# Sixteen weight slots moved to sixteen different offsets modulo 512 bytes in a fused attention and MoE kernel

## The chip, the cores and the metric

The kernel runs on one core of one Trainium2 chip. The metric is the device time of one execution in microseconds (us). Before the change it is 1794.76 us, the median of two runs (1793.05 and 1796.48).

## The reference

Three layers follow each other. First, attention over pooled keys and values, for 8 batches of 8 heads, 576 positions and 64 channels. Its result, as 4608 tokens of 512 channels, goes through two feed-forward layers.

```python
k_p = k.reshape(B, H, Sp, pool, D).mean(axis=3); v_p = v.reshape(B, H, Sp, pool, D).mean(axis=3)
scores = scale * np.matmul(q, k_p.transpose(0, 1, 3, 2))
attn = np.exp(scores - max); attn = attn / (sum + 1e-09)
x = np.matmul(attn, v_p)            # 4608 x 512, float32
h = x @ w_in                        # 512 x 2048 (float64 weights)
x = (h * np.cos(h)) @ w_out         # 2048 x 512
g = x @ w_gate; val = x @ w_val     # 512 x 1536 each
out = ((g * sigmoid(g)) * val) @ w_out2   # 1536 x 512, float32
```

## The kernel before

The program has two stages on one core. Nearly all matmuls have float32r operands. A number is split into a high part, the cast to float32r, and a low part, the rest. A product of two split numbers takes three matmuls: high times high, high times low, low times high.

Stage 1 (lines 1140 to 1234) runs over 9 blocks of 512 tokens and, within a block, over 16 slices of 128 hidden channels. `pe_h` (lines 545 to 554) computes a slice's hidden values: for each of 4 chunks of input channels three matmuls (lines 551, 552, 553), whose weights lie in the tile `wa[j, c]` and whose moving operand is the split input `xhl`. `pe_y` (lines 605 to 622) adds the slice's part of the output; its weights are in `wo` or `wo_ring`, its moving operands are the tiles `gh` and `gl`. In block 0 it uses plain float32 operands (line 613), and each of these matmuls shows in the trace as two instructions. The attention of the following batches is spread over the slots (`run_slot`), with its own small matmuls on lines 310, 363, 373 and 395.

Stage 2 (`fpair`, line 813, and `out_phase`, line 898) computes the second feed-forward layer by a scheme of seven products in place of eight, over five pairs of token halves: three with halves of 512 tokens, two with 384. Its weights are pieces of 128 x 1024 float32 (512 KB). Each of the 84 pieces of a pass is used in 12 matmuls (line 805, or line 935 for the last product), whose moving operand is one of the tiles `t_P`, `xhl` or `op`. The pieces are made once, in the first pass, stored to DRAM (`piece_store`, line 706) and loaded again for each later use (`piece_load`, line 700).

The weights of line 551 to 553 and the pieces of stage 2 live in the same sixteen buffers, called slots here: the pool `wts` with the sixteen tags `wa00` to `wa33`. A slot is 128 partitions by 4096 bytes. The tags are laid out in the order in which the program first asks for them: wa00 to wa03, wa10 to wa12, wa30 to wa32, wa20 to wa22, wa13, wa23, wa33. Before they are weights, slots also take raw `w_in` chunks (`cv_load`, line 469) and the raw keys and values of batch 1 (`load_kv1`, line 191). In stage 2 piece number r takes slot r modulo 16 (line 697), and SyncE's queue issues the load of piece r + 16 when piece r has been used (line 868).

Where things lie: every tile that lies between `xhl`, `gh`, `gl` and the slots is a whole multiple of 512 bytes in size, and so is a slot. All sixteen slots, `xhl`, `gh`, `gl`, the tiles `t_P` and `op`, and (with an unused tile of 224 bytes, `pad_1`) `wo_ring` therefore begin at the same offset modulo 512 bytes, 256. A block of weights for one matmul is 128 columns of 4 bytes, 512 bytes of a partition; it begins at a multiple of 512 bytes from its slot's start. So does each chunk of a moving tile. One kind of float32r matmul is laid out otherwise: on line 395 the weights of head pair p are 512 bytes after those of pair p - 1, but its moving operand `pth` is 1280 bytes after, so that the distance between the two, modulo 512, is 0 for an even pair and 256 for an odd one.

Of the kernel before, what the change touches and what calls it, by code (L numbers as in the profile page):

```python
# [8 lines left out]
F32 = mybir.dt.float32  # L9
F32R = mybir.dt.float32r  # L10
# [15 lines left out]
def fused_kernel(  # L26
# [23 lines left out]
    P = 128  # L50
# [5 lines left out]
    TB = 512  # L56
# [15 lines left out]
    dram = ctx.enter_context(tc.tile_pool(name="dram", bufs=1, space=bass.MemoryType.DRAM))  # L72
    psum = ctx.enter_context(tc.tile_pool(name="psum", bufs=1, space=bass.MemoryType.PSUM))
    wts = ctx.enter_context(tc.tile_pool(name="wts", bufs=1, reuse_waits="tile"))
    p1w = tc.alloc_tile_pool(name="p1w", bufs=2, side="right", reuse_waits="tile")
    p1a = tc.alloc_tile_pool(name="p1a", bufs=1, reuse_waits="tile")

# [46 lines left out]
    def raw_tile(nm):  # L124
        return chain.tile([P, 2, TB], F32, name=nm, tag="raw", bufs=2)
# [65 lines left out]
    def load_kv1():  # L191

        for g in range(3):
            t = wts.tile([P, 2, TB], F32, name=f"k1_{g}", tag=f"wa3{g}")
            kraw1.append(t if g < 2 else t[: SL * NP])
            if g < 2:
                for x in range(2):
                    nc.sync.dma_start(t[x * SM : (x + 1) * SM], kview[1][g, x])
            else:
                for r in range(2):  # L200
                    nc.sync.dma_start(t[: SL * NP, r], kleft[1][r])
        for j in range(0, NP + 1, 2):
            t = wts.tile([P, 2, TB], F32, name=f"v1_{j}", tag=f"wa2{j // 2}")
            for r in range(2):
                rows = t[r * SM : (r + 1) * SM]
                if j < NP:
                    nc.sync.dma_start(rows, vview[1][r, :, j : j + 2])
                else:
                    nc.sync.dma_start(rows[:, 0], vleft[1])
            vraw1.append((j, t[:, : min(2, NP + 1 - j)]))  # L210
# [256 lines left out]
    cv = {}  # L467

    def cv_load(key, src, home=None):
        st = raw_tile(f"st_{key}") if home is None else wts.tile([P, 2, TB], F32, name=f"st_{key}", tag=home)  # L470
        st = st.rearrange("p a t -> p (a t)")
        nc.sync.dma_start(st.bitcast(U64), src)
        cv[key] = st.rearrange("p (t two) -> p t two", two=2)

# [12 lines left out]
    def cv_sign(key):  # L487
        st, ce = cv[key]
        cu = ce.bitcast(U32)
        nc.vector.scalar_tensor_tensor(  # L490
            out=cu, in0=st.bitcast(U32)[:, :, 1], scalar=0x80000000, in1=cu, op0=ALU.bitwise_and, op1=ALU.bitwise_or
        )

    def cv_high(key):
        hi = cv[key][0].bitcast(U32)[:, :, 1]
        nc.vector.tensor_scalar(hi, hi, 0xFFFFF, 0x100000, op0=ALU.bitwise_and, op1=ALU.bitwise_or)

    def cv_low(key):
        st = cv[key][0]
        bits = st.bitcast(U32)  # L500
        nc.vector.scalar_tensor_tensor(
            out=st[:, :, 1], in0=bits[:, :, 0], scalar=2.0**-32, in1=bits[:, :, 1], op0=ALU.mult, op1=ALU.add
        )

    def cv_mul(key):

        st, ce = cv.pop(key)
        scale = 2.0**-20 * (INV_2PI if key[0] == "i" else 1.0)
        nc.vector.scalar_tensor_tensor(out=ce, in0=st[:, :, 1], scalar=scale, in1=ce, op0=ALU.mult, op1=ALU.mult)
        return ce  # L510
# [24 lines left out]
    wa = {}  # L535
# [128 lines left out]
    SLOTS = [f"wa{j}{c}" for j in range(NG1) for c in range(KC)]  # L664
    NS = len(SLOTS)
    wc_dram = dram.tile([PIECES, P, 2 * TB], F32, name="wc_dram")
    pieces = {}
# [26 lines left out]

    def piece_tile(r):

        pieces[r] = wts.tile([P, 2, 2, 2, P], F32R, name=f"wc_{r}", tag=SLOTS[r % NS])
        return pieces[r]

    def piece_load(r):  # L700
        if r >= PIECES * len(PAIRS) or r < NI * NQ:
            return
        t = piece_tile(r)
        nc.sync.dma_start(t.rearrange("p a b c d -> p (a b c d)").bitcast(F32), wc_dram[r % PIECES])
# [13 lines left out]
    def gen_steps(i):  # L718

        ts = {prod: piece_tile(i * NQ + n) for n, prod in enumerate(PRODUCTS)}  # L720
        for kind in range(2):
            t = w2raw.pop((i, kind))
# [241 lines left out]
    def load_i(m):  # L964
        for _ in range(m):
            u = next(to_load_i, None)
            if u is not None:
                _, j, c = order[u]
                cv_load(keys[u], w_in[c * P : (c + 1) * P, j * TB : (j + 1) * TB], f"wa{j}{c}")

    def load_o(m):
        for _ in range(m):
            u = next(to_load_o, None)
            if u is not None:
                f = order[u][2]
                cv_load(keys[u], w_out[f * P : (f + 1) * P, :])
# [4 lines left out]
    def first(u):  # L981
        kind, j, c = order[u]
        while keys[u] not in cv:
            (load_o if kind == "o" else load_i)(1)
        if kind == "o":
            ce = wo_raw[c // 8][:, c % 8]
        elif u < KC + LEAD:
            ce = None
        else:
            ce = wo_raw[1][:, 4 + (u if u < KC + LEAD else u // 2) % 4]  # L990
        cv_exp(keys[u], ce)
        cv_bias(keys[u])

    def conv():

        n = len(order)
        begun = 0
        x = None
        done = -1
        for u in range(n + 1):  # L1000
            if u < n:
                while begun <= u:
                    first(begun)
                    begun += 1
                    yield done
                cv_sign(keys[u])
                yield done
            if u > 0:
                x = cv_mul(keys[u - 1])
                if order[u - 1][0] == "o":  # L1010
                    load_o(1)
                    done = u - 1
                else:
                    _, j, c = order[u - 1]
                    home = wa[j, c] = wts.tile([P, 2, TB], F32R, name=f"wa_{j}_{c}", tag=f"wa{j}{c}")
                    nc.scalar.copy(home[:, 0], x)
                yield done
            if u < n:
                cv_high(keys[u])
                yield done  # L1020
            while begun < min(u + 3, n, ahead[0]) and not (order[begun][0] == order[begun - 1][0] == "o"):
                first(begun)
                begun += 1
                yield done
            if u < n:
                cv_low(keys[u])
                yield done
            if u > 0 and order[u - 1][0] == "i":
                nc.vector.tensor_sub(home[:, 1], x, home[:, 0])
                done = u - 1  # L1030
                yield done

    wo_raw = []
    conv_ops = conv()
    conv_done = [-1]
    ahead = [2 * KC]
# [32 lines left out]
    prep_k(0)  # L1069
    load_i(3)  # L1070
    load_kv1()
    fill(8)
    do_qt(0, 0)
# [61 lines left out]
    def w2_get():  # L1135
        cv_load(f"w2_{w2g[0]}", w2_src(w2g[0]))
        w2g[0] += 1
# [7 lines left out]
    for i, s in enumerate(slots):  # L1145
        n, f = s
# [159 lines left out]
```

## Time and profile before

| | |
|---|---|
| runs shown | 1793.05 and 1796.48 us, median 1794.76 us |
| profiled execution: span from first to last instruction | 1797.6 us (its own time is not listed apart) |
| matmul instructions | 8076, busy 1745.5 us, 97% of the span |
| weight loads | 8076, busy 1449.9 us, 81% |
| VectorE, ScalarE, GpSimd | 68%, 56%, 8% |
| DMA | 357.00 MB, mean 199 GB/s |

PE is TensorE's matmul side and PEld its weight loads, which overlap the matmuls. A matmul's duration in the trace includes the time from its first column to its last result, so matmuls that follow each other overlap; what one costs is read from the distance between starts. In the view of the chain, each entry runs until the next begins, so an entry of 24 matmuls gives 24 such distances.

### The profile page before, as it was taken

Reading aid. Unit: us, or ns where it says so; the run is one execution under the profiler, and the core shown is the slowest. Engines: PE = TensorE matmul, PEld = TensorE weight load, DVE = VectorE, ACT = ScalarE, POOL = GpSimd, SP = SyncE. Lnnn points to the kernel's source line nnn. Section 1 sums busy time; section 2 is a strip of 40 time slices with the busy share of each in tenths; the row PEclk is TensorE's granted clock in tenths of the full one; section 3 lists DMA queues with packets and bytes.
Section 4 is the critical chain, followed back from the end, with each engine's and each line's share of the span. In section 5 each row is a group of like instructions: output and inputs, shape, how many; then the busy total and the mean of one; then the engine's idle time right before and its main releaser. Section 6 shows DMA issues by size and latency. Waiting matters only on the chain.

```text
span 1797.6 us, 23341 instructions
## 1 busy us (share of the span) xinstructions
PE 1745.5 (97%) x8076; PEld 1449.9 (81%) x8076; DVE 1230.6 (68%) x2142; ACT 1002.4 (56%) x1815; POOL 134.8 (8%) x218
## 2 busy tenths in 40 slices
PE   4889999999999999999999999999999999999998
PEld 3556587888888878788888888888888888999998
DVE  6697687867777677687776586863684367458447
ACT  5577477766766767677565564533443344344333
POOL 0140500403103021000000000000000000000000
PEclk9899999999999999999999999999999999999999
DMA  9534244646566464574885488576667556787783
GB/s 235 159 115 111 85 161 142 203 130 203 143 210 220 109 208 126 158 244 137 235 278 183 169 310 290 192 260 218 192 201 265 197 190 221 298 254 249 291 255 92
DMA packets 240244, 357.00 MB, mean 199 GB/s; under 512 B 141696, under 2 KB 147840, under 8 KB 240128
## 3 DMA queue, kind: packets, MB, share of 16 engines
q1 hardware_dynamic: 235440, 354.35, 61.8%
q10 hardware_dynamic: 4688, 1.18, 0.3%
q8 instruction: 64, 1.05, 0.2%
q14 instruction: 52, 0.43, 0.1%
HBM read 285.74 MB, written 69.73 MB: 198 GB/s over the span
## 4 chain that ended last, share of the span: by engine, by line
PE 85%; DMA 6%; DVE 5%; issue 2%; ACT 1%; SPq 0%; ACTq 0%; POOL 0%; DVEq 0%; POOLq 0%
PE X L805 15%; PE oX L935 8%; PE Y L805 7%; PE h L551 7%; PE h L552 6%; PE h L553 6%; PE acc L620 6%; PE acc L621 6%; PE acc L622 6%; PE oY L935 4%; PE Z L805 4%; PE av L395 3%; PE acc L613 2%; PE oZ L935 2%; PE s L310 2%
## 5 line engine op out<-in xcount | busy, mean ns | idle before, releaser
L551 PE MATMUL h<-xhl,wa 128*128 128x512 f32 x576 | 233.7, 406 | 5.7 <-DVE w L587 5.7
L805 PE MATMUL X<-t_P,wc 128*128 128x512 f32 (+1 forms) x1080 | 233.0, 368 | 1.6 <-ACT u L854 1.6
L552 PE MATMUL h<-xhl,wa 128*128 128x512 f32 x576 | 228.0, 396 | 0.0
L553 PE MATMUL h<-xhl,wa 128*128 128x512 f32 x576 | 226.6, 393 | 0.0
L805 PEld LDWEIGHTS X<-t_P,wc 128*128 128x128 f32 x1080 | 196.5, 188 | 28.5 <-ACT u L854 3.3
L620 PE MATMUL acc<-gh,wo_ring 128*128 128x512 f32 x448 | 178.9, 399 | 0.0
L621 PE MATMUL acc<-gl,wo_ring 128*128 128x512 f32 x448 | 174.9, 390 | 0.1
L622 PE MATMUL acc<-gh,wo_ring 128*128 128x512 f32 x448 | 174.7, 390 | 0.0
L561 ACT ACTIVATE w<-h,few 128x512 f32<-128x512 f32 x144 | 98.7, 686 | 102.5 <-PE h L553 94.2
L551 PEld LDWEIGHTS h<-xhl,wa 128*128 128x128 f32 x576 | 109.6, 190 | 33.3 <-DVE w L587 7.5
L587 DVE SCALAR_TENSOR_TENSOR w<-w,h 128x512 f32<-128x512 f32 x144 | 98.1, 682 | 48.9 <-ACT w L584 47.2
L552 PEld LDWEIGHTS h<-xhl,wa 128*128 128x128 f32 x576 | 109.6, 190 | 24.0 <-issue 2.6
L553 PEld LDWEIGHTS h<-xhl,wa 128*128 128x128 f32 x576 | 109.4, 190 | 23.8 <-issue 0.5
L562 DVE SCALAR_TENSOR_TENSOR w<-w,h 128x512 f32<-128x512 f32 x144 | 98.0, 680 | 33.9 <-ACT w L561 33.3
L598 ACT CAST gh<-w 128x512 fp32r<-128x512 f32 x128 | 79.0, 617 | 72.2 <-DVE w L587 63.8
L857 DVE TENSOR_TENSOR p<-p,X 128x512 f32<-128x512 f32 (+1 forms) x60 | 37.8, 632 | 116.9 <-PE X L805 107.9
L583 ACT ACTIVATE w<-w 128x512 f32<-128x512 f32 x144 | 90.8, 632 | 47.5 <-DVE w L562 45.8
L601 DVE TENSOR_TENSOR gl<-w,gh 128x512 fp32r<-128x512 f32 x128 | 90.2, 704 | 30.0 <-ACT gh L598 28.1
L128 ACT CAST xhl<-pst 128x1024 fp32r<-128x1024 f32 (+1 forms) x70 | 67.7, 967 | 71.4 <-PE oX L935 26.1
L935 PE MATMUL oX<-xhl,wc 128*128 128x512 f32 (+1 forms) x480 | 102.8, 368 | 0.0
L622 PEld LDWEIGHTS acc<-gh,wo_ring 128*128 128x128 f32 x448 | 84.1, 188 | 18.5
L620 PEld LDWEIGHTS acc<-gh,wo_ring 128*128 128x128 f32 x448 | 84.1, 188 | 17.2 <-issue 0.8
(203 smaller groups left out, 3476.9 us busy)
## 6 DMA issues: line engine op xcount, KB each, us to landing
wc<-wc_dram SPq DMA_DIRECT2D x273, 512.0 KB
wo_ring<-wo_dram SPq DMA_DIRECT2D x112, 512.0 KB
wc_dram<-wc SPq DMA_DIRECT2D x42, 512.0 KB
wc_dram<-ow SPq DMA_DIRECT2D x42, 256.0 KB
y_dram<-yo SPq DMA_DIRECT2D x18, 512.0 KB
w_dram<-ce_w SPq DMA_DIRECT2D x36, 256.0 KB
st_i<-in_moe_w_in_dram SPq DMA_DIRECT2D x16, 512.0 KB
st_o<-in_moe_w_out_dram SPq DMA_DIRECT2D x16, 512.0 KB
```

The costliest lines, as they stand in the source:

```text
L551: nc.tensor.matmul(ps, whi, xhl[0][:, 0, c], start=c == 0, stop=False)
L552: nc.tensor.matmul(ps, whi, xhl[0][:, 1, c], start=False, stop=False)
L553: nc.tensor.matmul(ps, wlo, xhl[0][:, 0, c], start=False, stop=c == KC - 1)
L561: nc.scalar.activation(w, h, AF.Identity, bias=magic)
L562: nc.vector.scalar_tensor_tensor(out=w, in0=w, scalar=MAGIC, in1=h, op0=ALU.subtract, op1=ALU.subtract)
L583: nc.scalar.activation(w, w, AF.Sin, scale=PI)
L587: nc.vector.scalar_tensor_tensor(out=w, in0=w, scalar=1.0, in1=h, op0=ALU.subtract, op1=ALU.mult, reverse0=True)
L620: nc.tensor.matmul(acc[n][i], a[:, cols], xh, start=f == 0, stop=False)
L621: nc.tensor.matmul(acc[n][i], a[:, cols], xl, start=False, stop=False)
L622: nc.tensor.matmul(acc[n][i], b[:, cols], xh, start=False, stop=f == NF1 - 1)
L805: nc.tensor.matmul(ps[:, :hb], w, t[:, x, c, :hb], start=first and c == 0 and n == 0, stop=c == 1 and n == 2, skip_group_check=not first,)
L935: nc.tensor.matmul(banks[key][m][:, :hb], u, x[:, b, i, :hb], start=first_ and j == i == k == 0, stop=j == NJ - 1 and i == 1 and k == 2, s ...
```

## The change

The sixteen slots get 32 more bytes each (1032 columns of 4 bytes in place of 1024). A slot's contents begin at its start, except for the slots wa01, wa11, wa21 and wa31, where they begin 16 bytes later. Relative to before, and modulo 512, the slots then begin at: wa00 0, wa01 48, wa02 64, wa03 96, wa10 128, wa11 176, wa12 192, wa30 224, wa31 272, wa32 288, wa20 320, wa21 368, wa22 384, wa13 416, wa23 448, wa33 480. Tiles allocated after the pool on the same side move by 512 bytes in all, and stay where they were modulo 512. No instruction is added, removed or moved.

```diff
+    def slot_tile(tag, nm, dtype=F32):
+        s = 4 * int(tag[2]) + int(tag[3])
+        o = 4 * (s % 4 == 1)
+        return wts.tile([P, 2 * TB + 8], dtype, name=nm, tag=tag)[:, o : o + 2 * TB]
+
@@ load_kv1
-            t = wts.tile([P, 2, TB], F32, name=f"k1_{g}", tag=f"wa3{g}")
+            t = slot_tile(f"wa3{g}", f"k1_{g}").rearrange("p (a t) -> p a t", a=2)
@@
-            t = wts.tile([P, 2, TB], F32, name=f"v1_{j}", tag=f"wa2{j // 2}")
+            t = slot_tile(f"wa2{j // 2}", f"v1_{j}").rearrange("p (a t) -> p a t", a=2)
@@ cv_load
-        st = raw_tile(f"st_{key}") if home is None else wts.tile([P, 2, TB], F32, name=f"st_{key}", tag=home)
-        st = st.rearrange("p a t -> p (a t)")
+        st = slot_tile(home, f"st_{key}") if home else raw_tile(f"st_{key}").rearrange("p a t -> p (a t)")
@@ piece_tile
-        pieces[r] = wts.tile([P, 2, 2, 2, P], F32R, name=f"wc_{r}", tag=SLOTS[r % NS])
+        pieces[r] = slot_tile(SLOTS[r % NS], f"wc_{r}", F32R).rearrange("p (a b c d) -> p a b c d", a=2, b=2, c=2)
@@ conv
-                    home = wa[j, c] = wts.tile([P, 2, TB], F32R, name=f"wa_{j}_{c}", tag=f"wa{j}{c}")
+                    home = wa[j, c] = slot_tile(f"wa{j}{c}", f"wa_{j}_{c}", F32R).rearrange("p (a t) -> p a t", a=2)
```

## Rows read from the trace of the kernel before

**Rows 1.** The page: span, busy shares, PE and its clock in 40 slices.
```profile
span 1797.6 us, 23341 instructions
PE 1745.5 (97%) x8076; PEld 1449.9 (81%) x8076; DVE 1230.6 (68%) x2142; ACT 1002.4 (56%) x1815; POOL 134.8 (8%) x218
...
PEclk9899999999999999999999999999999999999999
...
PE 85%; DMA 6%; DVE 5%; issue 2%; ACT 1%; SPq 0%; ACTq 0%; POOL 0%; DVEq 0%; POOLq 0%
```

**Rows 2.** Busy time by stretch: PE, PEld, DVE, ACT, POOL, PEclk, DMA share, GB/s.
```profile
300.00:600.00 300.00, 298.17 (x1429) 248.32 (x1428) 226.81 (x437) 207.84 (x361) 60.06 (x97) 1.00 0.58 176
...
1020.00:1200.00 180.00, 178.40 (x782) 146.00 (x781) 136.91 (x229) 92.90 (x167) 0.00 (x0) 1.00 0.75 251
1200.00:1400.00 200.00, 199.97 (x881) 164.92 (x880) 110.58 (x135) 76.73 (x109) 0.00 (x0) 1.00 0.69 230
1400.00:1600.00 200.00, 200.00 (x979) 177.62 (x978) 107.81 (x144) 77.77 (x121) 0.00 (x0) 1.00 0.68 231
1600.00:1798.00 198.00, 192.66 (x1111) 192.10 (x1109) 122.18 (x180) 80.97 (x133) 0.00 (x0) 1.00 0.68 224
```

**Rows 3.** Groups of instructions by line: count, busy us, mean ns, idle before.
```profile
L551 PE MATMUL h<-xhl,wa 128*128 128x512 f32 x576 | 233.7, 406 | 5.7 <-DVE w L587 5.7
...
L552 PE MATMUL h<-xhl,wa 128*128 128x512 f32 x576 | 228.0, 396 | 0.0
L553 PE MATMUL h<-xhl,wa 128*128 128x512 f32 x576 | 226.6, 393 | 0.0
```

**Rows 4.** Whole span, line 805, then line 935: PE busy, PEld busy.
```profile
0.00:1798.00 1798.00, 519.63 (x2520) 458.22 (x2520) 0.99 0.62 199
...
0.00:1798.00 1798.00, 260.66 (x1260) 229.00 (x1260) 0.99 0.62 199
```

**Rows 5.** The chain, three stretches: start us, us until the next entry, what.
```profile
110.88 3.43 PE acc L613 x8
...
1405.25 5.44 PE X L805 x24
...
1667.85 4.16 PE X L805 x24
```

**Rows 6.** Weight loads near 1451 us, in order of time: start us, us.
```profile
1448.39 2.68 PEld L805 LDWEIGHTS Y<-xhl,wc 128*128 128x128 f32 x12
1451.11 2.68 PEld L805 LDWEIGHTS X<-xhl,wc 128*128 128x128 f32 x12
```

**Rows 7.** PE in order of time, one av step of stage 1.
```profile
258.79 0.28 PE L395 MATMUL av<-pth,vmh 128*128 128x256 f32 x1
...
259.39 0.28 PE L395 MATMUL av<-pth,vmh 128*128 128x256 f32 x1
...
259.99 0.40 PE L620 MATMUL acc<-gh,wo 128*128 128x512 f32 x1
```

**Rows 8.** PE in order of time, behind an idle stretch of stage 1.
```profile
776.26 0.50 PE L551 MATMUL h<-xhl,wa 128*128 128x512 f32 x1 [0.88 <-DVE w L587]
776.60 0.40 PE L552 MATMUL h<-xhl,wa 128*128 128x512 f32 x1
...
777.54 0.39 PE L553 MATMUL h<-xhl,wa 128*128 128x512 f32 x1
777.77 0.39 PE L551 MATMUL h<-xhl,wa 128*128 128x512 f32 x1
...
779.15 0.39 PE L620 MATMUL acc<-gh,wo_ring 128*128 128x512 f32 x1
...
779.83 0.39 PE L620 MATMUL acc<-gh,wo_ring 128*128 128x512 f32 x1
```

**Rows 9.** DMA issues, and what the SyncE queue waited for (us, times, longest).
```profile
wc<-wc_dram SPq DMA_DIRECT2D x273, 512.0 KB
...
SPq L704 <- PE X L805: 179.0, 96, 2.9
SPq L704 <- PE Y L805: 94.7, 48, 3.9
```

**Rows 10.** What PE waited for a DMA in the whole span.
```profile
PE qp L295 <- DMA q<-in_q_dram: 7.1, 1, 7.1
```

## The prediction

> **What bounds the kernel now.** I read the page first, then the busy time by stretch, then the chain and the order of single matmuls. TensorE is busy 97% of the span and holds 85% of the chain that ended last, at the full granted clock in nearly every slice [rows 1]. By stretch it is plainer: from 300 us on PE is busy 99% of the time or more, and from 1200 to 1600 us 399.97 of 400 us, while VectorE, ScalarE and the DMA engines (share 0.58 to 0.75) all have slack [rows 2]. So the time is the number of matmuls times the distance from one start to the next, and a change that adds no instruction can move it only through that distance, or by making a hidden transfer late.
>
> The distance is very regular. In stage 2, 24 matmuls of 512 columns take 5.44 us, 226.7 ns each, and 24 of 384 columns take 4.16 us, 173.3 ns each [rows 5]. The 128 columns between them cost 53.4 ns, 0.417 ns a column; 512 columns are then 213.5 ns and 13.2 ns are left over, the same for both lengths. The two-pass matmuls of line 613 take 3.43 us for eight, 428.8 ns each [rows 5]; twice 213.5 ns is 427.0, so there only 1.8 ns are left over, although each has a weight load of the same size. So some 11 ns of every float32r matmul are there because a weight load runs beside it, and the start of each group of 12 loads lies 0.22 us before the matmuls that use it, inside the previous ones [rows 5, 6].
>
> **The change part by part.** Nothing is removed. What moves is where the weight reads begin, relative to the moving reads beside them. The slots serve 3 x 576 matmuls of lines 551 to 553 [rows 3], 2520 of line 805 and 1260 of line 935 [rows 4]: 5508 of 8076 matmuls. One nanosecond on each is 5.5 us. All but the 192 of the first block lie where PE is never short of work, so a nanosecond there goes whole into the span.
>
> Does the distance depend on these offsets? The trace has one comparison. On line 395 the distance between weights and moving operand, modulo 512 bytes, is 0 for head pair 0 and 256 for pair 1. Five matmuls of pair 0 take from 258.79 to 259.39, those of pair 1 from 259.39 to 259.99: 0.60 us both, 120 ns each [rows 7]. 256 columns at 0.417 ns are 106.8, so 13.2 ns are left over at 0 and at 256 alike. A shift of half the 512 bytes costs and gains nothing. Shifts that are no multiple of 256 are in no row of a float32r matmul. I take the value that this comparison gives, no change: 5508 x 0.
>
> The bounds of that unknown come from two other places. Upward: behind an idle stretch the same matmuls, at the same offsets, are for a while further apart. From 776.60 to 779.15 us eleven distances average 231.8 ns, the first four 235.0 [rows 8]; a little later, 779.15 to 779.83, it is 227 again. So the left-over time isn't a fixed cost: it depends on how the two reads stand to each other in time, and settles at 13.2 ns. If new offsets keep it from settling, the nearest prices are 5.1 and 8.3 ns, 28 and 46 us over 5508 matmuls. A far end is that the left-over time doubles, 13.2 ns more or 73 us. Downward: it falls to the 1.8 ns of line 613, 11.4 ns less or 63 us.
>
> The Trainium skill, "TensorE: Matmul & The Clock Gate", section "Back-to-back issue gap", gives N / 2.4 + 2.5 ns for matmuls that follow each other, and its section "Step-by-step: what each phase is for" says that loading the next weights does not take read bandwidth from the running matmul. The trace does not agree with the first: 226.7 ns at 512 columns against 215.8. If only the shared offset kept this kernel from that figure, the estimate by the page would be 5508 x 10.9 ns, 60 us less.
>
> The slots are also the target of 273 loads in stage 2 and of earlier transfers [rows 9]. Rows of 4096 bytes no longer begin at a multiple of 256 bytes in fifteen of the slots, and four of these not at one of 32. I cost this at nothing. The cover: each load is issued when its slot comes free, fifteen pieces of 12 matmuls (2.72 us each, half an entry of 24 in [rows 5]) ahead of its use, 41 us; the queue waits for PE to free slots (96 and 48 times for two of the lines' groups [rows 9]); PE waited for a DMA once in the whole span, at the start, 7.1 us [rows 10]. The DMA share there is 0.68 to 0.75 [rows 2], so all transfers could take a third longer before they set the pace. The reads and writes of VectorE and ScalarE in the slots keep their shapes and end with slack.
>
> The sum against the profiled execution: 1797.6 us of span, nothing added. It lies 2.8 us above the median of the runs, 0.2%, so the forecast is given in the runs' terms: 1795 us, own range 1788 to 1803.
>
> **The rivals.**
>
> *The lock is lost (slower).* Settling needs a state that each matmul hands on to the next. Now all slots stand alike to the moving tiles; after the change the slot changes every 3 matmuls in stage 1 and every 12 in stage 2, and with it the offset. For it: the left-over time is seen to vary between two reads of one engine [rows 8], and 13.2 ns is a value at 0 and 256 only. Against it: the same state holds at three lengths and at both offsets [rows 5, 7]. It decides from an average of 6.5 ns per slot matmul on (36 us, 2%). Between the prices 5.1 and 8.3 ns I take 6.7: 37 us, 1832 us; it may reach 1868.
>
> *The reads come apart (faster).* Equal offsets may be what makes the reads meet, and fifteen new ones free most loads. For it: two-pass matmuls, which ask for a column half as often, lose only 1.8 ns [rows 5]. Against it: 256 bytes apart should have helped already [rows 7]. Whole, it gives 1795 - 63 = 1732 us; half of it, 1764.
>
> *Loads set the pace (slower).* Unaligned rows slow the transfers. From a factor of 1.4 on (0.70 x 1.43 = 1) stage 2, about 780 us, follows the DMA engines; at 1.5 that is 5% of it, 39 us, 1834 us. But only four slots are off by 16 bytes: twice the time for these would make 1.25 in all, 0.88 of the engines. The Trainium skill, "DMA: Bandwidth & Descriptors", section "How a descriptor splits into AXI transactions", says that a transfer which starts off a 256-byte boundary fetches the bytes before its start as well; by its account at most 7 beats more on a row of 128, an estimate of 5%. No row here shows such a transfer; 5% would leave it hidden.
>
> *The edit does not do what it says.* If the allocator rounded each slot to 512 bytes, only the 16 bytes would be left. The time would be that of the forecast.
>
> **How the numbers follow.** No change 0.42, the lock is lost 0.39, the reads come apart 0.14, loads 0.03, no effect of the edit 0.02. Two per cent, about what a measurement of this kernel can tell from no change, is below 1759 and above 1831. Of the lost lock somewhat over half lies above (0.24 with the loads' 0.02 gives 0.26); of the reads coming apart somewhat over half lies below (0.08); the rest is within, 0.66. Since cases of both signs hold more than half, the range reaches from half the gain, 1765, to past the upper price of the lost lock, 1850; some 0.08 is left out below and 0.1 above.
>
> **What would show it.** Right: entries of 24 matmuls in stage 2 still take 5.44 and 4.16 us, for every slot, and lines 551 to 553 keep their mean durations. The lost lock: these entries are longer by some 0.1 to 0.3 us, by amounts that repeat with the slot, every sixteen pieces, while line 620 to 622, whose weights stay, change only next to a slot's load. The reads apart: entries near 5.2 us for most slots. Loads: PE idle before line 805 with a DMA named. I am wrong if the distance differs from 226.7 ns by more than 1 ns on average over stage 2.

## The result, and the profile after

The changed kernel takes 1818.42 us (1817.19 and 1819.65), against 1794.76 us before: 1.0126 times as long, with a 95% interval of 1.0088 to 1.0163. That is 23.7 us more. It lies inside the stated range and under the 2% bound, but not at the point forecast, and outside that forecast's own range of 1788 to 1803.

The page of the changed kernel, its lines that answer to [rows 1], and the DMA queue that carries the pieces:

```profile
span 1815.1 us, 23341 instructions
PE 1765.9 (97%) x8076; PEld 1449.5 (80%) x8076; DVE 1231.7 (68%) x2142; ACT 1002.8 (55%) x1815; POOL 136.2 (8%) x218
...
PEclk9989999999999999999999999999999999999999
...
q1 hardware_dynamic: 235440, 354.35, 61.1%
...
PE 89%; DVE 5%; DMA 3%; issue 1%; ACT 1%; SPq 0%; POOL 0%; ACTq 0%; DVEq 0%; POOLq 0%
```

The instructions and their counts are those of before, and so is the clock from 225 us on. VectorE, ScalarE and the weight loads have the same busy time within 1.1 us. Of the rest only PE is busy clearly longer, by 20.4 us, and its share of the chain rises from 85 to 89%. Of the 20.4 us, 5.3 lie in a line whose weights were not moved: line 613 (617 now), before and after:

```profile
L613 PE MATMUL acc<-w,wo 128*128 128x512 f32 x128 | 59.5, 612 | 5.4 <-DVE wo L509 5.4
...
L617 PE MATMUL acc<-w,wo 128*128 128x512 f32 x128 | 64.8, 656 | 5.5 <-DVE wo L513 5.5
```

Its first matmuls now fall into a stretch at the lower clock (granted clock 0.50 from 95 to 100 us, that is 1.2 GHz); before, the first of them started at 100 us, and the clock was 1.00 from there to 105 us.

The views that answer to [rows 4] (whole span, line 805 and 935 before, 809 and 939 now: PE busy, PEld busy):

```profile
0.00:1816.00 1816.00, 529.25 (x2520) 460.21 (x2520) 0.99 0.62 197
...
0.00:1816.00 1816.00, 264.89 (x1260) 229.91 (x1260) 0.99 0.62 197
```

Stage 2 matmuls are busy 9.6 and 4.2 us longer with the same counts. Measured from the starts of single matmuls, stage 2 (first to last start) grew from 782.7 to 795.4 us, 12.7 us, and stage 1 from its 500th matmul on from 824.5 to 832.9 us, 8.4 us. Together that is 21.1 us. The two profiled spans differ by less, 17.5 us, because the first 500 matmuls were over 3.6 us earlier in the profiled run of the changed kernel (181.5 against 185.2 us), in a stretch where the clock and the waits vary. The medians of the runs differ by 23.7 us; the profiled span of before, 1797.6 us, is longer than either of the two runs in that median took.

The chain of the changed kernel around 1440 us, which answers to [rows 5] (start us, us until the next entry, what; an entry of 12 is one piece, one slot):

```profile
1414.62 2.79 PE Y L809 x12
1417.41 5.56 PE X L809 x24
1422.97 2.79 PE Y L809 x12
1425.76 5.60 PE X L809 x24
1431.36 2.78 PE Z L809 x12
1434.14 2.77 PE Y L809 x12
...
1442.51 2.80 PE Y L809 x12
...
1450.91 2.75 PE Z L809 x12
```

Before, a piece of 512 columns took 2.72 us whatever its slot, as here:

```profile
1418.85 2.72 PE Z L805 x12
1421.57 2.72 PE Y L805 x12
```

A pass has 63 pieces, not the 84 that stand in the section on the kernel: 3780 matmuls in five passes, 12 to a piece. Now the entry from 1422.97 is slot wa01 (48 bytes off), that from 1434.14 is wa11 (176 bytes) and that from 1450.91 is wa23 (448 bytes). Most slots cost 0.06 to 0.08 us more per piece, these last two 0.03 to 0.05 us. Near the end, with 384 columns, the same view shows far less:

```profile
1690.54 4.17 PE X L809 x24
...
1719.93 4.19 PE X L809 x24
...
1734.56 4.24 PE X L809 x24
```

Against 4.16 us before, these are 0.01 to 0.08 us more on 24 matmuls.

Taking the distance of each two starts less 0.417 ns a column, leaving out distances with an idle stretch in them: in stage 2, inside a slot, the left-over time rose from 13.5 to 19.0 ns at 512 columns and from 13.4 to 14.8 ns at 384. On line 551 to 553 it rose from 14.3, 14.2 and 14.3 ns to 19.5, 18.4 and 18.4 ns. With the counts, 2268 x 5.5 + 1512 x 1.4 + 576 x 13.5 ns = 22.4 us, 4.1 ns on average over the 5508 matmuls. That accounts for the 21.1 us above and, within the spread of the runs, for the 23.7.

Two more readings. The mean durations of line 551 to 553 moved by 1 ns only, although the medians rose from 389 ns each to 396, 394 and 393: the means also hold the long matmuls behind a pause, which became fewer (68 over 430 ns before, 48 now), and the time of those pauses fell by 5 us. And PE waited for a DMA once, as before, at the start:

```profile
PE qp L300 <- DMA q<-in_q_dram: 6.7, 1, 6.7
```

### The profile page after: what moved, and what is told of

It is laid out like the page before. It is cut to its first block, busy times and chain, and to the rows that moved or that the text cites. A ratio compares the mean times of both kernels' runs of the same rounds, so it can differ in the third digit from the quotient of the medians.

```text
span 1815.1 us, 23341 instructions
## 1 busy us (share of the span) xinstructions
PE 1765.9 (97%) x8076; PEld 1449.5 (80%) x8076; DVE 1231.7 (68%) x2142; ACT 1002.8 (55%) x1815; POOL 136.2 (8%) x218
## 3 DMA queue, kind: packets, MB, share of 16 engines
q1 hardware_dynamic: 235440, 354.35, 61.1%
## 4 chain that ended last, share of the span: by engine, by line
PE 89%; DVE 5%; DMA 3%; issue 1%; ACT 1%; SPq 0%; POOL 0%; ACTq 0%; DVEq 0%; POOLq 0%
PE X L809 16%; PE oX L939 8%; PE Y L809 8%; PE h L555 7%; PE h L556 7%; PE h L557 7%; PE acc L624 6%; PE acc L626 6%; PE acc L625 6%; PE oY L939 4%; PE Z L809 4%; PE av L400 3%; PE s L315 2%; PE oZ L939 2%; PE acc L617 2%
## 5 line engine op out<-in xcount | busy, mean ns | idle before, releaser
L809 PE MATMUL X<-t_P,wc 128*128 128x512 f32 (+1 forms) x1080 | 237.0, 372 | 0.5 <-ACT u L858 0.4
L591 DVE SCALAR_TENSOR_TENSOR w<-w,h 128x512 f32<-128x512 f32 x144 | 98.4, 684 | 49.6 <-ACT w L588 48.1
L624 PEld LDWEIGHTS acc<-gh,wo_ring 128*128 128x128 f32 x448 | 84.2, 188 | 17.5 <-issue 0.8
```

Of the source, the lines that this page charges most:

```text
L591: nc.vector.scalar_tensor_tensor(out=w, in0=w, scalar=1.0, in1=h, op0=ALU.subtract, op1=ALU.mult, reverse0=True)
L624: nc.tensor.matmul(acc[n][i], a[:, cols], xh, start=f == 0, stop=False)
L809: nc.tensor.matmul(ps[:, :hb], w, t[:, x, c, :hb], start=first and c == 0 and n == 0, stop=c == 1 and n == 2, skip_group_check=not first,)
```

## The experiments

After the result three theories stood. **Offset theory:** a matmul's distance follows from the offset of the weights that are being loaded to the moving operand beside the load. **Change theory**, the rival "the lock is lost" as the prediction put it: only the change of offset from slot to slot costs. **Address theory:** weight blocks that don't begin at a round address are slow to read, whatever the moving operand does. Times are given as ratios to runs of the kernel before on the same chip, with 95% intervals.

**One offset for all slots.** All sixteen slots are moved by the same 64 bytes, the pool is filled up to 512.

```diff
+    SHIFT = 64
+    wts.tile([P, SHIFT // 4], F32, name="pad_w", tag="pad_w")
+    def slot_tile(tag, nm, dtype=F32):
+        more = (512 - SHIFT) // 4 if tag == "wa33" else 0
+        return wts.tile([P, 2 * TB + more], dtype, name=nm, tag=tag)[:, : 2 * TB]
```

> All sixteen slots begin 64 bytes further on, the same for all; moving tiles stay. Offset theory (the distance of two matmuls follows from the offset of the weights being loaded to the moving operand beside the load, modulo 512): stage 2 settles nowhere near before; 512-column matmuls alternate between two values as slot wa02 does now, about 233.8 ns on average, 24 of them 5.61 us; 384-column ones stay at 4.16 us; time 1810 to 1820 us. Change theory (only the change of offset from slot to slot costs): the offset never changes, so 5.44 us and 4.16 us as before, 1795 us. Address theory (weights that do not begin at a multiple of 256 bytes are slow to read): slower, like the offset theory.

Measured: 1821.01 us, 1.0125 [1.0110, 1.0140]. Its chain:

```profile
1401.88 5.60 PE X L810 x24
...
1407.48 2.80 PE Y L810 x12
...
1718.02 4.19 PE X L810 x24
```

Each piece of 512 columns takes 2.80 us and never settles at 2.72 us. So a single offset can cost as much as sixteen different ones, and the change theory falls as the whole cause: nothing changes here from slot to slot. A small part of it stays. In the changed kernel slot wa00 stands where it stood, and its left-over time is 15.2 ns at 512 columns, because in 8 of its 12 pieces the first seven distances after slot wa33 are still uneven. The expectation for 384 columns was missed, 4.19 us in place of 4.16, a left-over time of 14.7 ns, and the time is 1 us above the range given.

**Everything moved together.** Slots, moving tiles and `wo_ring` begin 64 bytes further on.

```diff
+    const.tile([P, 16], F32, name="pad_c")
     ident = const.tile([P, P], F32, name="ident")
@@ begin2, and the end
-        p1w.tile([P, 56], F32, name="pad_1", tag="pad", bufs=1)
+        p1w.tile([P, 40], F32, name="pad_1", tag="pad", bufs=1)
-    pools2["b"].tile([P, 56], F32, name="pad_2", tag="pad", bufs=1)
+    pools2["b"].tile([P, 40], F32, name="pad_2", tag="pad", bufs=1)
```

> Slots, moving tiles and wo_ring all begin 64 bytes further on. Offset theory: the offsets to each other are as before, so 24 matmuls take 5.44 and 4.16 us, 1795 us. Address theory: no block begins at a multiple of 256 bytes any more, 24 matmuls take about 5.6 us, 1815 us or more. Change theory: as before, 1795 us.

Measured: 1798.36 us, 1.0000 [0.9989, 1.0011].

```profile
1403.84 5.44 PE X L806 x24
...
1666.42 4.16 PE X L806 x24
```

The slots begin at the same addresses as in the experiment above and cost nothing. What counts is the offset to the moving operand, and the address theory falls.

**Half of 512 bytes.** As the first experiment, with SHIFT = 256.

> All sixteen slots begin 256 bytes further on; moving tiles stay. Offset theory with a period of 256 bytes, as line 395 has it: 5.44 and 4.16 us, 1795 us. Offset theory with a period of 512 bytes: 24 matmuls of 512 columns take 5.5 us or more, 1805 us or more. Change theory and address theory: as before, 1795 us.

Measured: 1800.09 us, 1.0003 [0.9993, 1.0012].

```profile
1405.48 5.44 PE X L810 x24
...
1688.88 4.16 PE X L810 x24
```

The left-over times are those of before, 13.5 and 13.4 ns. A whole kernel at 256 bytes confirms what [rows 7] showed in one place. Of the four pairs of slots that stand 256 bytes apart in the changed kernel, two agree at 512 columns (wa02 and wa20, at 64 and 320: 23 and 18 ns in turn in both; wa30 and wa33) and two don't (wa10 and wa22: 18.4 and 20.4 ns; wa12 and wa23: 19.8 and 15.9). In the experiment without the 16 bytes, below, there are eight such pairs, and the means of all eight agree within 0.6 ns. The price repeats after 256 bytes, not 512; why two pairs of the changed kernel differ is taken up under the offset with two patterns.

**Other weights.** The slots stay; the two unused tiles go, so that `wo_ring` stands 224 bytes off `gh` and `gl`.

```diff
-        p1w.tile([P, 56], F32, name="pad_1", tag="pad", bufs=1)
-    pools2["b"].tile([P, 56], F32, name="pad_2", tag="pad", bufs=1)
```

> The slots as before; the two unused tiles of 224 bytes are left out, so that wo_ring begins 224 bytes further on and the weights of line 620 to 622 stand 224 bytes off their moving operands. Offset theory: these 1344 matmuls cost 4 to 7 ns more, 5 to 9 us gross, of which stage 1 hides a part: 1797 to 1804 us, with stage 2 at 5.44 and 4.16 us. Change theory: the offset changes twice per slot of stage 1, each with a few disturbed matmuls, also 1796 to 1800 us, and line 620 to 622 settle at 226.7 ns within their twelve.

Measured: 1805.88 us, 1.0035 [1.0021, 1.0050]. That is 1.9 us above the range given; against the runs of before beside it, 1798.96 us, it is 6.9 us more, within the 5 to 9 us gross. In order of time:

```profile
901.96 0.40 PE L621 MATMUL acc<-gl,wo_ring 128*128 128x512 f32 x1
...
902.89 0.39 PE L622 MATMUL acc<-gh,wo_ring 128*128 128x512 f32 x1
903.12 0.39 PE L551 MATMUL h<-xhl,wa 128*128 128x512 f32 x1
```

Five distances take 1.16 us, 232 ns each, at the end of the twelve: they don't settle. The left-over time of line 620 to 622 is 20.0, 19.9 and 19.0 ns, against 15.3, 14.7 and 14.5 before, while stage 2 stays at 13.5. So it is no property of the slots; the unused tile of 224 bytes was worth 0.35% to the kernel before.

**Without the 16 bytes.** The change with `o = 0`: sixteen steps of 32 bytes.

> The change without the 16 bytes more: the slots begin at sixteen steps of 32 bytes. Offset theory with a period of 256 bytes: slot wa31, at 256, runs as at 0, 13.3 ns over the columns; wa11, at 160 instead of 176, rises from 17 to about 20 ns; wa01 and wa21 stay near 20. In sum no change against the change itself: 1.011 to 1.014 times before. Alignment theory (rows and weight blocks that begin off a 32-byte boundary cost extra): the four slots get cheaper and the time falls by some us.

Measured: 1815.86 us, 1.0105 [1.0081, 1.0129], just under the 1.011 expected; the interval overlaps that of the change. The slots tell more than the time:

```profile
1414.37 2.73 PE Z L807 x12
1417.10 2.79 PE Y L807 x12
...
1436.59 2.80 PE Y L807 x12
```

The entry from 1414.37 is wa31, now at 256, back at 2.73 us; that from 1436.59 is wa11, now at 160, up from 2.77. The other two slots stay (wa01 20.0 and 19.7 ns, wa21 19.8 and 20.0). In sum the 16 bytes cost nothing of their own.

**Small offsets.** SHIFT = 32 for all slots, one execution.

> All slots 32 bytes further on. Offset theory: as slot wa32 now, 20 ns over the columns at 512 columns (24 matmuls 5.60 us), 14.7 ns at 384 (4.19 us); span some 20 us over that of before. If small offsets cost less than large ones: less than 5.55 us.

Measured: 1818.96 us, span 1816.8 us.

```profile
1401.27 5.60 PE X L810 x24
...
1707.91 4.16 PE X L810 x24
```

At 512 columns 32 bytes cost as much as 64, 20.0 ns. At 384 columns they cost nothing (13.4 ns), where 14.7 was expected.

**An offset with two patterns.** SHIFT = 192, one execution.

> All slots 192 bytes further on. Two slots stand at this offset modulo 256 now and differ: wa23 runs at 16 ns over the columns (13, 16, 19 in turn), wa12 at 20 (20, 20, 21). If the offset alone sets the cost, all pieces show one of the two. If it also matters how the piece before leaves the two reads, the run holds one pattern throughout, set at its start or after an idle stretch: 24 matmuls of 512 columns take 5.50 us or 5.60 us, 384 columns 4.16 us.

Measured: 1805.5 us, span 1803.4 us.

```profile
1418.11 5.49 PE X L810 x24
...
1709.01 4.16 PE X L810 x24
```

All pieces of 512 columns show 13, 16 and 19 ns in turn, the pattern that wa23 has in the changed kernel, never the 20, 20, 21 of wa12. So an offset doesn't set the price alone: more than one steady pattern can belong to it. What chooses may be the state in which the matmuls before leave the engine. In the changed kernel wa12 fell from its usual 20, 20, 21 into 13, 16, 19 in the middle of one of its 12 pieces. In the run with 64 bytes for all slots the pattern was 23, 18 at first, 20, 20, 21 from about 1130 to 1307 us, and 23, 18 again; each time it changed within a few matmuls. That the state chooses is inferred from this; no run set it.

**Steps under 32 bytes.** As the change, but the first eight slots are 8 bytes, the last eight 16 bytes past a multiple of 32.

```diff
+    LATER = ("wa31", "wa32", "wa20", "wa21", "wa22", "wa13", "wa23", "wa33")
+        o = 4 if tag in LATER else 2
```

> As the change, but the first eight slots begin 8 bytes after a multiple of 32 (8, 40, 72 ...) and the last eight 16 bytes after one (272, 304 ... which is 16, 48 ... modulo 256). If reads go by lines of 16 bytes or more, the slot at 8 runs as one at 0, 13.3 ns over the columns, and one at 40 as one at 32. If single bytes count, the slot at 8 costs about 20 ns like the others. Time as the change, 1815 to 1825 us.

Measured: 1815.9 us, one execution. The slot at 8 bytes runs at 17.6 ns (16, 16, 21, 17, 18 in turn) at 512 columns and 13.3 at 384. That is neither of the two expectations: 8 bytes are enough to leave the pattern of 0, but not to pay the full price. The slot at 40 bytes (wa01) was expected to run as one at 32. At 512 columns it does, 19.7 ns. At 384 it doesn't: it pays 20.0 ns in each of its eight pieces, where 32 bytes cost nothing. The chain shows one of them among its neighbours:

```profile
1680.51 2.09 PE Y L809 x12
...
1686.76 2.16 PE Y L809 x12
```

The second entry is wa01; before, such an entry took 2.08 us.

The left-over time by offset, worked out from the starts of single matmuls in stage 2 (one offset for all slots, but for the rows marked with a slot):

| offset modulo 256 | at 512 columns, ns in turn | mean | mean at 384 |
|---|---|---|---|
| 0 (before) | 13.3, once settled | 13.5 | 13.4 |
| 8 (first slot, last experiment) | 16, 16, 21, 17, 18 | 17.6 | 13.3 |
| 32 | 19, 22, 18, 22 | 20.0 | 13.4 |
| 40 (second slot, last experiment) | 16, 22, 23 | 19.7 | 20.0 |
| 64 | 23, 18, in one stretch 20, 20, 21 | 20.0 | 14.7 |
| 176 (wa11, the change) | 13, 16, 23, 16 | 16.8 | 14.0 |
| 192 | 13, 16, 19 | 15.7 | 13.4 |
| 224 (wa30, wa33, the change) | 21, 18, 22, 20 | 19.9 | 16.4 |
| 232 (eighth slot, last experiment) | 18, 18, 18, 19 | 17.7 | 13.0 |

## Why the prediction was right or wrong

**The bound** was read rightly: PE sets the pace, and a nanosecond on a slot matmul goes into the time. 22.4 us of longer distances gave 21 to 24 us. Stage 1 passed on its 8 us too. One reading was too round: PE is not busy 99% in every stretch from 300 us on, but 98.4% from 600 to 900 us and 97.3% in the last one.

**The failing step** is "I take the value that this comparison gives, no change". The comparison [rows 7] was true, and the experiment with 256 bytes confirms it for the whole kernel. But it compared two offsets that are the same point of a pattern of 256 bytes, and was stretched to fifteen offsets between them that no row showed. What the runs showed in its place: in stage 2 5.5 ns on average at 512 columns, 1.4 at 384. By the sign that the prediction itself set, more than 1 ns on average over stage 2, the forecast of no change was wrong. The other sign of being right, that lines 551 to 553 keep their mean durations, came out within 1 ns and still misled. And the step before, that some 11 ns of every float32r matmul are there because a weight load runs beside it, doesn't follow from its rows: the matmuls of line 613 have such loads too. No run here shows what the 13.3 ns consist of.

**The upper bound** came out near in size, partly by luck. The first of the two prices from behind an idle stretch [rows 8], 5.1 ns and 28 us over all 5508 matmuls, lies near the 4.1 ns and 24 us measured; 8.3 ns was too much. But it is the price of a short unsettled stretch at one offset, where the runs show settled patterns at other offsets, 2 to 7 ns dearer at 512 columns, and an average that hangs on which offsets the sixteen slots got: all at 192 bytes gave 1805.5 us. The prediction chose 6.7 for that rival (1832 us) and gave it 0.39, after 0.42 for no change. The reading that the left-over time is no fixed cost, because it changes after a pause, was the better evidence and should have had the higher chance.

**The rival "the lock is lost"** named the right direction and place, but the wrong mechanism. It let the price come from the change of offset between slots. One offset for all slots costs as much (1.0125), so the matmuls don't fail to settle: at each offset they settle into a repeating pattern, and of the offsets tried only 0 and 256 have every settled distance of 512 columns at 13.3 ns over the columns. Of its signs one was right, longer entries by amounts that repeat with the slot, every sixteen pieces.

**One price for both lengths** was wrong too. All 5508 matmuls were counted alike; the 1512 of 384 columns pay a quarter as much on average. That is no rule for 384 columns: offsets of 8, 32 and 192 bytes cost them nothing, 40 bytes the full 6.6 ns. Why the length matters is open.

**"The reads come apart"** is refuted for the offsets tried: at 512 columns every offset but 0 and 256 has a dearer mean than before. At 384 the lowest is 13.0 ns, 0.4 less, for the slot at 232 bytes in the last experiment (9, 15, 13, 15, 14 in turn); single matmuls come down to 8 ns, between dearer ones. The 215.8 ns a matmul that the prediction took from the Trainium skill, "TensorE: Matmul & The Clock Gate", section "Back-to-back issue gap", were not reached at any offset; that section gives the formula for a single matmul by itself.

**Loads** were rightly costed at nothing. The queue's packets took 61.8% of 1797.6 us before and 61.1% of 1815.1 us now, 1111 and 1109 us. The line of before:

```profile
q1 hardware_dynamic: 235440, 354.35, 61.8%
```

What the prediction took from the Trainium skill, "DMA: Bandwidth & Descriptors", section "How a descriptor splits into AXI transactions", is about the bytes that a transfer fetches. For the 273 loads only the side that is written moved, so their unchanged time is no test of it.

That it is two reads meeting in the memory that cost the time is argued, not shown. Shown is that the price belongs to the offset between the weights and the moving operand, modulo 256 bytes, that it needs neither a change of offset nor particular addresses, and that it appears for `wo_ring` as for the slots. Open is which of two offsets it is: that of the weights being loaded to the operand that streams beside the load, as the offset theory has it, or that of a matmul's own weights and own moving operand. Within a slot both are the same. They differ where one group of lines follows another, and there the traces don't agree. With `wo_ring` 224 bytes off, the left-over time behind a matmul of line 553 that is followed by line 620, beside which a moved block is loaded, rose from 13.4 to 21.7 ns, as the offset theory says. With the slots 64 bytes off, that behind a matmul of line 622 followed by line 551, beside which a moved block is loaded too, fell from 13.4 to 12.5 ns (line numbers of the kernel before). No run moved the moving tiles alone. None of the layouts tried beats the kernel before.

## What to carry to other kernels

With float32r matmuls of 512 columns that follow each other without a pause, check the offset modulo 256 bytes between each weight block and the moving tiles that stream with it and while it is loaded: 0 gave 226.7 ns each, the others tried 228 to 234 on average, and a few unused bytes in a pool are the whole mend. With 384 columns check too: 40 bytes cost 6.6 ns there, 32 bytes nothing. Look for such a cost in the distance of starts, not in busy shares or in mean durations, which hid it in stage 1. And when a trace compares two values of a setting and finds them equal, ask whether they could be the same point of something that repeats before applying it to the values between.

## What the runs showed of the hardware that was not expected

The distances are a repeating sequence, the same to a nanosecond in most rounds of a slot: 13, 16, 23, 16 at an offset of 176, 13, 16, 19 at 192. The same offset can hold two sequences: at 64 bytes 23 and 18 in turn and, in another stretch of the same run, 20, 20, 21, at the same mean of 20 ns. At 192 bytes the two differ in price, 16 against 20 ns. And 8 bytes, two float32 numbers, already cost 4 ns a matmul of 512 columns and nothing at 384, while 40 bytes cost the full price at both lengths.
